# Reordering an attention and feed-forward kernel: every half pair begins with contexts, sums of weights earlier, GpSimd's additions later, the last scores between contexts

## The chip, the cores and the metric

The kernel runs on one core of a Trainium2 chip. A core has five engines that run side by side, each with a queue of instructions that it takes in order: TensorE (PE in the profile, with its weight loads as PEld), VectorE (DVE), ScalarE (ACT), GpSimd (POOL) and SyncE (SP, which here issues DMA transfers). An instruction that waits for another engine holds up everything behind it in its own queue. TensorE writes to PSUM, a small memory of eight banks; VectorE and ScalarE read it from there; GpSimd works on SBUF, the large on-chip memory. The metric is the device time of one execution in microseconds (us). Before the change it is 927.66 us, the median of three runs (926.39 to 928.1).

## The reference

Rows x (2048 rows of 640) are normalised, and the result xn goes two ways that are joined at the end. All tensors are bfloat16.

```python
xn = _layernorm(x, axis=-1)
q = (xn @ wq).reshape(B, Sq, 32, 192).transpose(0, 2, 1, 3)
k = k_cache[:, :, Sk - 512:, :]          # the last 512 keys of each of 32 heads
v = v_cache[:, :, Sk - 512:, :]
scores = jnp.einsum("bhqd,bhkd->bhqk", q, k) * (192 ** -0.5)
o = jnp.einsum("bhqk,bhkd->bhqd", _softmax(scores, axis=-1), v)
s = o.transpose(0, 2, 1, 3).reshape(B, Sq, 32 * 192) @ wo
g = _silu((_silu(xn @ w_gate) * (xn @ w_up)) @ w_down)
return x + s * g
```

## The kernel before

The feed-forward part with its result g comes first (to about 165 us). What follows is attention, in 16 *pairs* of heads, numbered 0 to 15 (`pr`). The 2048 queries are cut into four *blocks* of 512, and a pair is done in two *halves* of two blocks each. A block of a pair has the number i = 4 * pair + block. The order of the work on each engine is written out by hand: instructions run in the order in which the Python code issues them.

**Scores phase** (`scores_phase`, L924). A half begins with eight scores, two blocks by four chunks of 128 keys (`scores`, L592). A score is six matmuls into a PSUM tile `sc` (of which there are two, used in turn), and an exponential on ScalarE (L601) that empties it into `p_t`. Between the scores, at numbered slots 0 to 7, stand the products that make the queries of the *next* half: `differences`, `sides`, `across`, `sums` and `third` (`q_group`, L554). They use two more PSUM tiles, `mm`, which VectorE or ScalarE empties. The third product of a block is reduced by VectorE at L534 (`q_rows`). `sides` ends in a copy on ScalarE (L573); `across` adds on VectorE (L576), then subtracts at L581, on GpSimd for the pairs 0 to 14 and on VectorE for pair 15; `sums` ends at L586. In the first half of a pair two more things prepare the next pair: `combine_wq` (L136, three VectorE instructions at L143 that add and subtract weights) at slot 5, and `q_diag` (L548) at slot 7, a product that needs one of those sums and whose PSUM tile VectorE copies out at L552.

**Beside it** (`beside`, L905) run the preparations of the next pair's keys: transposing DMAs in the first half; in the second, sums over keys on VectorE (L174) at slots 0 to 2, and the *key centring* (`centre_k`, L180: five VectorE instructions at L186 that write `khat`) at slots 4 to 7.

**Stretch.** After the scores of a half comes a stretch of two kinds of work, in an order written as a string (`FIRST`, `LATER`, L884). Each name has a block of the half (0 and 1, or 2 and 3), a letter and a step 0 or 1:

- a and b are *contexts*, the products of `p_t` with the values (`pv`, L604), a for the first two query tiles of a block and b for the other two. They accumulate in an `mm` tile, taken at step 0. Each step is 16 matmuls of 64 rows, of which two run at once in two halves of the array. Between the steps the halves change PSUM banks, which is kept in order by a one-element `turn_t` memset in GpSimd's queue (L726): step 1 waits for it. After step 1 `divide` (L636) takes reciprocals on VectorE (L641), divides on ScalarE (L652; some parts on VectorE, L646) and issues a transposing DMA (L655).
- w, x and y are the *output products* with wo for the block two before, i - 2 (`wo_units`, L781): w0, w1, x0, x1 (`wo_turn`, L733, also with a turn between its steps) and y0 (`rest`). They use `sc` tiles, which VectorE adds to the running sums s_m and s_t (L752).

The first half of a later pair begins 0a0 0b0 0y0 0x0; its second half begins 2w0 2a0 2w1 2b0. Pair 0 has orders of its own.

**The end.** Pair 14 has no such string: `pv_full` and `wo_full` (L660, L808) do contexts and output products with matmuls of 128 rows. After the output product `gate` multiplies finished sums by g on GpSimd (L768), and `add_x` (L770, L779) adds x, in three instructions for each block: block 2 after the first half of pair 14, block 3 right after the scores of its second half, block 0 after the scores of pair 15's first half, all on GpSimd; block 1 on VectorE. Pair 15 does the scores of blocks 0 and 1 as above. Those of blocks 2 and 3 (s20 to s33) stand between the contexts of blocks 0 and 1 as `LAST` says. Then `pv_full`, `last_rows` and `last_rest` alternate until the stores.

Of the kernel before, what the change touches and what calls it, by code (L numbers as in the profile page):

```python
# [15 lines left out]
def kernel(  # L16
# [28 lines left out]
    NB = Sq // 512  # L45
# [90 lines left out]
    def combine_wq(pr):  # L136

        w = pairs[pr]["wq"]
        wc = pairs[pr]["wc"] = w[:, :, :, :].bitcast(h16)
        for to, a, b, op in (  # L140
            (TOTAL, SWAP, OTHER, ALU.add), (SWAP, SWAP, OWN, ALU.add), (OTHER, OTHER, OWN, ALU.subtract)
        ):
            nc.vector.tensor_tensor(wc[:, to, :, :], w[:, a, :, :], w[:, b, :, :], op)  # L143
# [57 lines left out]
    with ExitStack() as fctx:  # L201
# [238 lines left out]
        for b in range(NB):  # L440
# [3 lines left out]
            u = 0  # L444
# [72 lines left out]
    last = NPAIR - 1  # L517
    Ps, OTs, Obs, xbs = {}, {}, {}, {}
# [85 lines left out]
    def pv(i, q2):  # L604

        pr, b = divmod(i, NB)
        st = {}

        def part(p):
            if p == 0:  # L610
                if i not in OTs:
                    Obs[i] = opool.tile([P, 4, 2, Dh], bf, name="O_b")
                    tag = "OT_l" if late(i) and pr < last else "OT_b"
                    OTs[i] = otpool.tile([P, 12, P], bf, name=tag, tag=tag, bufs=2 if tag == "OT_l" else 3)
                st["acc"] = sc_tile() if i < 2 and q2 else mm_tile()
            acc = st["acc"]
            turn, h = divmod(p, 2)
            for kc in range(KC):
                for n, r in enumerate((lo, hi)):
                    k = n ^ turn  # L620
                    qt = 2 * q2 + k
                    m = nc.tensor.matmul(  # L622
                        acc[:, k, h * 256 : h * 256 + Dh + 1],
                        Ps[i][kc][r, h, qt * P : (qt + 1) * P], V_p[r, kc, h, 0 : Dh + 1],
                        start=(p == 0 and kc == 0), stop=(turn == 1 and kc == KC - 1),
                        skip_group_check=True,
                    )
                    after(m, st)
            if p == 1:
                turned(m, st)  # L630
            if p == 3:
                divide(i, q2, acc, (0, 1) if q2 == i else (0,) if pr == last else ())

        return [lambda t=t: (part(2 * t), part(2 * t + 1)) for t in range(2)]

    def divide(i, q2, acc, by_dve):  # L636
        pr, b = divmod(i, NB)
        O_b, OT_b = Obs[i], OTs[i]
        r = smpool.tile([P, 2, 2, 1], f32, name="r")
        a_v = acc[:, :, :].rearrange("p k (h c) -> p k h c", h=2)  # L640
        nc.vector.reciprocal(r[:], a_v[:, :, :, Dh : Dh + 1])  # L641
        for k in range(2):
            qt = 2 * q2 + k
            a_k = a_v[:, k, :, :]
            if by_dve and k in by_dve:
                nc.vector.tensor_tensor(  # L646
                    O_b[:, qt, :, :], a_k[:, :, 0:Dh], r[:, k, :, :].to_broadcast([P, 2, Dh]),
                    ALU.mult,
                )
                continue  # L650
            for h in range(2):
                nc.scalar.activation(  # L652
                    O_b[:, qt, h, :], a_k[:, h, 0:Dh], ACT.Copy, scale=r[:, k, h, :]
                )
        nc.sync.dma_start_transpose(  # L655
            out=OT_b[:, 6 * q2 : 6 * q2 + 6, :],
            in_=O_b[:, 2 * q2 : 2 * q2 + 2, :, :].rearrange("p t h d -> p (t h d)"),
        )

    def pv_full(i, q2):  # L660

        pr, b = divmod(i, NB)
        if q2 == 0:
            Obs[i] = opool.tile([P, 4, 2, Dh], bf, name="O_b")
            tag = "OT_l" if late(i) and pr < last else "OT_b"
            OTs[i] = otpool.tile([P, 12, P], bf, name=tag, tag=tag, bufs=2 if tag == "OT_l" else 3)
        O_b, OT_b = Obs[i], OTs[i]
        alone = pr == last and 2 * b + q2 < 5
        acc = mm_tile()
        for k in range(2):  # L670
            qt = 2 * q2 + k
            for h in range(2):
                for kc in range(KC):
                    nc.tensor.matmul(  # L674
                        acc[:, k, h * 256 : h * 256 + Dh + 1],
                        Ps[i][kc][:, h, qt * P : (qt + 1) * P], V_p[:, kc, h, 0 : Dh + 1],
                        start=(kc == 0), stop=(kc == KC - 1),
                    )
        divide(i, q2, acc, alone and (0,))

    def load_xb(b):

# [87 lines left out]
    def add_x(b, eng):  # L770
        for qts in (slice(0, 2), slice(2, 4), None):
            add_part(b, qts, eng)
# [8 lines left out]
    def wo_units(i):  # L781


        pr, b = divmod(i, NB)

        def unit(half):
            st = {}

            def first():
                st["sc"] = sc_tile()  # L790
                wo_turn(st, i, half, 0)

            def second():
                wo_turn(st, i, half, 1)
                sum_rows(i, slice(2 * half, 2 * half + 2), st["sc"][:, :, :])

            return [first, second]

        def rest():
            sc = sc_tile()  # L800
            for n, r in enumerate((lo, hi)):
                wo_rest(sc[:, n, :], i, r)
            for n in range(2):
                add_sum(pr + n, s_t[:, b, :], sc[:, n, :])

        return [unit(0), unit(1), [rest]]
# [72 lines left out]
    def store(left):  # L879
# [1 line left out]
            t, ob = stores.pop(0)  # L881
            nc.sync.dma_start(out=out2[t * P : (t + 1) * P, :], in_=ob)

    FIRST = ("0a0 0b0 0a1 0b1 1a0 1b0 1a1 1b1", "2a0 2b0 2w0 2w1 2a1 2y0 2x0 2b1 2x1 3w0 3a0 3w1 3b0 3y0 3a1 3x0 3b1 3x1")  # L884
    LATER = (
        "0a0 0b0 0y0 0x0 0a1 0x1 0w0 0b1 0w1 1w0 1b0 1w1 1a0 1b1 1y0 1x0 1a1 1x1",
        "2w0 2a0 2w1 2b0 2a1 2y0 2x0 2b1 2x1 3w0 3b0 3w1 3a0 3b1 3y0 3x0 3a1 3x1",
    )
    LAST = "s20 0a0 s21 0b0 0a1 0b1 s22 1a0 s23 1b0 s30 1a1 s31 1b1 s32 s33"

    def units_of(pr, bs):
        units = {}
        for b in bs:
            i = pr * NB + b
            units.update({"%da" % b: pv(i, 0), "%db" % b: pv(i, 1)})
            if i >= 2 and pr < last:
                units.update({"%d%s" % (b, n): u for n, u in zip("wxy", wo_units(i - 2))})
        return units

    def stretch(pr, half):  # L900
        units = units_of(pr, (2 * half, 2 * half + 1))
        for name in (LATER if pr else FIRST)[half].split():
            units[name[:2]][int(name[2])]()

    def beside(pr, n):  # L905
# [18 lines left out]
    def scores_phase(pr, half):  # L924


        nxt = pr + 1 < NPAIR
        if half == 0 and pr == 0:
            work = [lambda i=i, j=j: q_rows(i, j) for i in (2, 3) for j in range(3)]
            slots = {0: work[0:1], 1: work[1:2], 3: work[2:3], 4: work[3:4], 5: work[4:5], 6: work[5:6]}  # L930
        elif half == 0 or nxt:
            of = pr if half == 0 else pr + 1
            differences, sides, across, sums, third = q_group(of, 1 - half)
            slots = {
                0: [differences], 1: [sides], 3: [across, lambda: third(0)], 4: [sums],
                6: [lambda: third(1)],
            }
        if half == 0 and nxt:
            slots.setdefault(7, []).append(lambda: q_diag(pr + 1))
            slots.setdefault(5, []).insert(0, lambda: combine_wq(pr + 1))  # L940
        for n in range(2 * KC):
            for do in slots.get(n, ()):
                do()
            scores(pr * NB + 2 * half + n // KC, n % KC)
            beside(pr, 2 * half * KC + n)
            if pr >= last - 1 and (pr, half, n) in XB_AT:
                load_xb(XB_AT[pr, half, n])

    XB_AT = {(last - 1, 0, 7): 2, (last - 1, 1, 0): 3, (last - 1, 1, 4): 0, (last, 0, 0): 1}
    V, G = nc.vector, nc.gpsimd  # L950

    for pr in range(last):
        for half in range(2):
            scores_phase(pr, half)
            if pr == last - 1 and half:
                add_x(3, G)
            if pr < last - 1:
                stretch(pr, half)
                continue
            for b in (2 * half, 2 * half + 1):  # L960
                i = pr * NB + b
                for q2 in range(2):
                    pv_full(i, q2)
                    wo_full(i - 2, q2)
            if half == 0:
                add_x(2, G)
# [1 line left out]
    add_x(0, G)  # L968
    add_x(1, V)
    i = last * NB  # L970
    units = units_of(last, (0, 1))
    for name in LAST.split():
        if name[0] == "s":
            scores(i + int(name[1]), int(name[2]))
# [3 lines left out]
        m_f[:, 0, :, :], m_f[:, 1, :, :],  # L978
        xc[:, SUM + 1, 0:4, :].rearrange("p c n -> p (c n)").bitcast(f32).rearrange("p (t d) -> p t d", d=512),
    ]  # L980
    pv_full(i + 2, 0)
    for b, q2, more in ((0, 0, (2, 1)), (0, 1, (3, 0)), (1, 0, (3, 1)), (1, 1, None)):
        last_rows(b, slice(2 * q2, 2 * q2 + 2), G, sc_tile)
        if q2:
# [47 lines left out]
```

## Time and profile before

| | |
|---|---|
| median of three runs | 927.66 us (926.39 to 928.1) |
| the profiled execution | 927.22 us |
| its span, first to last instruction | 925.4 us |
| busy, TensorE | 905.7 us (98%) |
| busy, VectorE | 583.3 us (63%) |
| busy, ScalarE | 501.6 us (54%) |
| busy, GpSimd | 148.5 us (16%) |
| mean granted TensorE clock | 0.998 |
| one pair (2 to 13), start to start | 46.9 us |

Busy time of TensorE includes the pipelined tail of each matmul, so rows overlap: a row of six score matmuls shows 0.83 us, but the row behind it starts 0.65 us after it. Where TensorE has work waiting, six matmuls of 64 rows by 512 columns take 0.65 us from start to start of rows, ten 1.08 us, a context step (x16) 0.67 us and two of them (x32) 1.33 us. With this a wait is read from the starts of two rows in the timeline: what lies between them, less what the first needs.

### The profile page before, as it was taken

The numbers are of one execution on the slowest core, as the hardware profiler recorded it, in microseconds if no ns is written. First come the engines' busy times: TensorE is split into PE (matmuls) and PEld (weight loads), VectorE is DVE, ScalarE is ACT, GpSimd is POOL, SyncE is SP. The second block draws the span as 40 slices with busy tenths as digits, with TensorE's granted clock in tenths as the row PEclk, the third lists the DMA queues.
The fourth block names the chain that finished last, engine by engine and source line by source line (L and its number), as shares of the span: only waits on it lengthen the run. The fifth ranks groups of instructions, "written<-read, shape, count | busy, mean of one in ns | idle before, by whom it ended". The sixth has DMA issues, their size and how long they took to land.

```text
span 925.4 us, 23283 instructions
## 1 busy us (share of the span) xinstructions
PE 905.7 (98%) x9797; PEld 539.4 (58%) x9819; DVE 583.3 (63%) x862; ACT 501.6 (54%) x873; POOL 148.5 (16%) x298
## 2 busy tenths in 40 slices
PE   9999999999999999999999999999999999999898
PEld 5444444465656666666666666666665666665565
DVE  6443552465767676767676767676766676767657
ACT  4222222566656566656566666666656656566471
POOL 0000000011111111111111111111111111116826
PEclk9999999999999999999999999999999999999999
DMA  9313460054444444455444444444444453544336
GB/s 301 75 35 91 97 123 0 1 91 88 81 85 81 92 81 91 81 91 83 91 81 91 81 91 81 91 82 91 77 88 85 76 94 78 91 80 111 67 87 163
DMA packets 266025, 81.98 MB, mean 89 GB/s; under 512 B 244928, under 2 KB 265920, under 8 KB 265920
## 3 DMA queue, kind: packets, MB, share of 16 engines
q1 hardware_dynamic: 263552, 77.82, 42.5%
q10 hardware_dynamic: 2368, 2.67, 0.9%
q8 instruction: 77, 1.26, 0.6%
q14 instruction: 28, 0.23, 0.1%
HBM read 41.39 MB, written 2.62 MB: 48 GB/s over the span
## 4 chain that ended last, share of the span: by engine, by line
PE 82%; DVE 7%; ACT 3%; DMA 2%; issue 2%; POOL 2%; SPq 1%; DVEq 0%; ACTq 0%; POOLq 0%
PE mm L622 15%; PE sc L739 15%; PE sc L597 11%; PE sc L315 11%; PE mm L543 9%; PE mm L345 6%; PE mm L529 5%; PE sc L709 4%; PE sc L701 2%; DVE wq_p L143 2%; PE mm L674 2%; DVE qT L534 2%; ACT p_t L601 2%; DVE m_f L552 2%; POOL m_f L581 2%
## 5 line engine op out<-in xcount | busy, mean ns | idle before, releaser
L601 ACT ACTIVATE p_t<-sc 128x1024 bf16<-128x1024 f32 x256 | 253.9, 1025 | 81.5 <-PE sc L597 81.3
L652 ACT ACTIVATE O_b<-mm,r 128x192 bf16<-128x192 f32 x490 | 166.2, 422 | 198.6 <-issue 125.4
L597 PE MATMUL sc<-qT,khat 64*128 64x512 bf16 x1536 | 197.4, 376 | 1.2 <-ACT p_t L601 1.2
L622 PEld LDWEIGHTS <-p_t 64*128 64x128 bf16 x3712 | 164.6, 94 | 39.3 <-issue 4.0
L622 PE MATMUL mm<-V_p,p_t 64*128 64x193 bf16 x3648 | 184.9, 243 | 1.7 <-ACT O_b L652 0.4
L739 PE MATMUL sc<-wo_p,OT_b 64*128 64x512 bf16 x1296 | 171.3, 376 | 7.1 <-ACT p_t L601 6.8
L752 DVE TENSOR_TENSOR s_m<-s_m,sc 128x1024 f32<-128x1024 f32 x108 | 131.9, 1221 | 71.4 <-PE sc L739 63.3
L597 PEld LDWEIGHTS <-khat 64*128 64x128 bf16 x1536 | 87.4, 94 | 78.4 <-issue 1.8
L739 PEld LDWEIGHTS <-OT_b 64*128 64x128 bf16 x1296 | 69.5, 94 | 54.5 <-issue 11.0
L726 POOL MEMSET turn_t<- 128x1 f32 x224 | 22.2, 99 | 477.5 <-PE mm L622 249.4
L752 DVE TENSOR_TENSOR s_t<-s_t,sc 128x512 f32<-128x512 f32 x108 | 74.2, 687 | 38.8 <-PE sc L709 36.9
L534 DVE TENSOR_REDUCE qT<-mm 128x512 bf16<-128x1024 f32 x66 | 80.6, 1222 | 26.2 <-PE mm L529 23.3
L543 PE MATMUL mm<-xc,wq_p 64*128 64x512 f16 x750 | 94.2, 376 | 0.4 <-ACT O_b L652 0.4
L581 POOL TENSOR_TENSOR m_f<-m_f 128x1024 f32<-128x1024 f32 x28 | 65.8, 2349 | 178.4 <-DVE qT L576 172.1
L543 PEld LDWEIGHTS <-wq_p 64*128 64x128 f16 (+1 forms) x1050 | 56.3, 94 | 58.2 <-DVE wq_p L143 5.1
L529 PE MATMUL mm<-xnT,wq_p 64*128 64x512 bf16 x660 | 82.9, 376 | 0.2 <-ACT m_f L573 0.2
L323 DVE TENSOR_TENSOR hT<-sc,sg 128x512 bf16<-128x512 f32 x46 | 31.7, 691 | 70.2 <-ACT sg L322 70.2
L576 DVE TENSOR_TENSOR qT<-mm,m_f 128x1024 bf16<-128x1024 f32 x30 | 36.7, 1224 | 56.6 <-ACT m_f L573 56.6
L322 ACT ACTIVATE sg<-sc 128x512 bf16<-128x512 f32 x46 | 27.3, 597 | 69.8 <-PE sc L315 65.1
L315 PE MATMUL sc<-xnT,wg_sb 128*128 128x512 bf16 (+1 forms) x255 | 59.9, 354 | 1.4 <-DMA wg_sb<-in_B_w_gate_dram 0.7
L315 PE MATMUL sc<-xnT,wu_sb 128*128 128x512 bf16 (+1 forms) x255 | 59.4, 354 | 0.2
L529 PEld LDWEIGHTS <-wq_p 64*128 64x128 bf16 x660 | 35.9, 94 | 37.1 <-issue 5.7
(96 smaller groups left out, 720.6 us busy)
## 6 DMA issues: line engine op xcount, KB each, us to landing
wo_p<-in_A_wo_dram SPq DMA_DIRECT2D x16, 480.0 KB, 3.8
wq_p<-in_A_wq_dram SPq DMA_DIRECT2D x79, 80.0 KB, 2.9
K_p<-in_A_k_cache_dram SPq DMA_DIRECT2D x32, 192.0 KB, 3.1
V_p<-in_A_v_cache_dram SPq DMA_DIRECT2D x32, 192.0 KB, 3.1
wq_p<-in_A_wq_dram SPq DMA_DIRECT2D x90, 40.0 KB, 2.6
x_t<-in_A_x_dram SPq DMA_DIRECT2D x13, 160.0 KB, 2.9
xc<-in_A_x_dram SPq DMA_DIRECT2D x4, 512.0 KB, 4.3
OT_b<-O_b SPq DMA_TRANSPOSE x124, 2.8
```

What stands on the lines that cost most here:

```text
L315: nc.tensor.matmul(out, w_sb[:, c, f * P : (f + 1) * P], xnT[:, c, qc], start=(c == 0), stop=(c == NC - 1),)
L345: nc.tensor.matmul(dn, at, by, start=(f == 0), stop=(f == NF - 1))
L529: nc.tensor.matmul(q_ps[:, h, :], w[r, AS_IS[j], c, :], xnT[r, c, b * 512 : (b + 1) * 512], start=(c == 0), stop=(c == NC - 1),)
L534: nc.vector.reduce_sum(q_of(i, j), q_ps[:, :, :].rearrange("p h n -> p n h"), axis=AX.X)
L543: nc.tensor.matmul(ps[:, h, :], ws[h][r, c, :], xs[h][r, c, :], start=(first and c == 0), stop=(c == NC - 1), skip_group_check=True,)
L581: eng.tensor_tensor(m_f[:, SIDE_S, :, :], diag, m_f[:, SIDE_S, :, :], ALU.subtract)
L597: nc.tensor.matmul(sc[:, h, :], khat[r, j, ks], q_of(i, j)[r, :], start=(j == 0), stop=(j == 2))
L601: nc.scalar.activation(p_t[:, :, :], sc[:, :, :], ACT.Exp, scale=scale)
L622: m = nc.tensor.matmul(acc[:, k, h * 256 : h * 256 + Dh + 1], Ps[i][kc][r, h, qt * P : (qt + 1) * P], V_p[r, kc, h, 0 : Dh + 1], start=(p ...
L652: nc.scalar.activation(O_b[:, qt, h, :], a_k[:, h, 0:Dh], ACT.Copy, scale=r[:, k, h, :])
L739: m = nc.tensor.matmul(ps[:, k, :], OTs[i][r, 3 * (2 * half + k) + j, :], pairs[i // NB]["wo"][r, j, MAIN], start=(turn == 0 and j == 0), ...
L752: nc.vector.tensor_tensor(to, to, ps, ALU.add)
```

## The change

Both halves of every later pair, and the second half of pair 0, use the one order that the first half had, which begins with contexts; `combine_wq` goes from slot 5 to slot 2 of the first half; `add_x(3, G)`, three GpSimd instructions, goes from ahead of pair 14's last contexts and output products to a place between them, behind the first `gate`; `LAST` begins with a context instead of a score, and takes the first contexts of block 2 in two steps, one ahead of the last score and one behind it, where `pv_full(i + 2, 0)` had followed all scores. The same computation is done with the same instructions, but for those contexts, which become 32 matmuls of 64 rows and one more memset in place of 16 of 128 rows.

```diff
--- before.py
+++ after.py
@@ -660,12 +660,11 @@
     def pv_full(i, q2):
 
         pr, b = divmod(i, NB)
-        if q2 == 0:
+        if i not in OTs:
             Obs[i] = opool.tile([P, 4, 2, Dh], bf, name="O_b")
             tag = "OT_l" if late(i) and pr < last else "OT_b"
             OTs[i] = otpool.tile([P, 12, P], bf, name=tag, tag=tag, bufs=2 if tag == "OT_l" else 3)
         O_b, OT_b = Obs[i], OTs[i]
-        alone = pr == last and 2 * b + q2 < 5
         acc = mm_tile()
         for k in range(2):
             qt = 2 * q2 + k
@@ -676,7 +675,7 @@
                         Ps[i][kc][:, h, qt * P : (qt + 1) * P], V_p[:, kc, h, 0 : Dh + 1],
                         start=(kc == 0), stop=(kc == KC - 1),
                     )
-        divide(i, q2, acc, alone and (0,))
+        divide(i, q2, acc, ())
 
     def load_xb(b):
 
@@ -881,25 +880,22 @@
             t, ob = stores.pop(0)
             nc.sync.dma_start(out=out2[t * P : (t + 1) * P, :], in_=ob)
 
-    FIRST = ("0a0 0b0 0a1 0b1 1a0 1b0 1a1 1b1", "2a0 2b0 2w0 2w1 2a1 2y0 2x0 2b1 2x1 3w0 3a0 3w1 3b0 3y0 3a1 3x0 3b1 3x1")
-    LATER = (
-        "0a0 0b0 0y0 0x0 0a1 0x1 0w0 0b1 0w1 1w0 1b0 1w1 1a0 1b1 1y0 1x0 1a1 1x1",
-        "2w0 2a0 2w1 2b0 2a1 2y0 2x0 2b1 2x1 3w0 3b0 3w1 3a0 3b1 3y0 3x0 3a1 3x1",
-    )
-    LAST = "s20 0a0 s21 0b0 0a1 0b1 s22 1a0 s23 1b0 s30 1a1 s31 1b1 s32 s33"
-
-    def units_of(pr, bs):
+    FIRST = "0a0 0b0 0a1 0b1 1a0 1b0 1a1 1b1"
+    LATER = "0a0 0b0 0y0 0x0 0a1 0x1 0w0 0b1 0w1 1w0 1b0 1w1 1a0 1b1 1y0 1x0 1a1 1x1"
+    LAST = "0a0 s20 0b0 s21 0a1 0b1 s22 1a0 s23 1b0 s30 1a1 s31 1b1 s32 2a0 s33 2a1"
+
+    def units_of(i, n):
         units = {}
-        for b in bs:
-            i = pr * NB + b
-            units.update({"%da" % b: pv(i, 0), "%db" % b: pv(i, 1)})
-            if i >= 2 and pr < last:
-                units.update({"%d%s" % (b, n): u for n, u in zip("wxy", wo_units(i - 2))})
+        for k in range(n):
+            units.update({"%da" % k: pv(i + k, 0), "%db" % k: pv(i + k, 1)})
+            if 2 <= i < last * NB:
+                units.update({"%d%s" % (k, n): u for n, u in zip("wxy", wo_units(i + k - 2))})
         return units
 
     def stretch(pr, half):
-        units = units_of(pr, (2 * half, 2 * half + 1))
-        for name in (LATER if pr else FIRST)[half].split():
+        i = pr * NB + 2 * half
+        units = units_of(i, 2)
+        for name in (LATER if i else FIRST).split():
             units[name[:2]][int(name[2])]()
 
     def beside(pr, n):
@@ -937,7 +933,7 @@
             }
         if half == 0 and nxt:
             slots.setdefault(7, []).append(lambda: q_diag(pr + 1))
-            slots.setdefault(5, []).insert(0, lambda: combine_wq(pr + 1))
+            slots.setdefault(2, []).append(lambda: combine_wq(pr + 1))
         for n in range(2 * KC):
             for do in slots.get(n, ()):
                 do()
@@ -952,8 +948,6 @@
     for pr in range(last):
         for half in range(2):
             scores_phase(pr, half)
-            if pr == last - 1 and half:
-                add_x(3, G)
             if pr < last - 1:
                 stretch(pr, half)
                 continue
@@ -961,6 +955,8 @@
                 i = pr * NB + b
                 for q2 in range(2):
                     pv_full(i, q2)
+                    if b == 2 and q2:
+                        add_x(3, G)
                     wo_full(i - 2, q2)
             if half == 0:
                 add_x(2, G)
@@ -968,7 +964,7 @@
     add_x(0, G)
     add_x(1, V)
     i = last * NB
-    units = units_of(last, (0, 1))
+    units = units_of(i, 3)
     for name in LAST.split():
         if name[0] == "s":
             scores(i + int(name[1]), int(name[2]))
@@ -978,7 +974,6 @@
         m_f[:, 0, :, :], m_f[:, 1, :, :],
         xc[:, SUM + 1, 0:4, :].rearrange("p c n -> p (c n)").bitcast(f32).rearrange("p (t d) -> p t d", d=512),
     ]
-    pv_full(i + 2, 0)
     for b, q2, more in ((0, 0, (2, 1)), (0, 1, (3, 0)), (1, 0, (3, 1)), (1, 1, None)):
         last_rows(b, slice(2 * q2, 2 * q2 + 2), G, sc_tile)
         if q2:
```

## The prediction

> **What bounds the kernel now.** I read the page first, for whether one engine carries the whole span.
>
> ```profile
> PE 905.7 (98%) x9797; PEld 539.4 (58%) x9819; DVE 583.3 (63%) x862; ACT 501.6 (54%) x873; POOL 148.5 (16%) x298
> PE   9999999999999999999999999999999999999898
> ```
>
> TensorE is the bound in every slice, and VectorE and ScalarE have a third to a half of their time free. What can be gained without taking matmuls away is the time in which TensorE waits, so I went through its timeline and compared the starts of rows with the 0.65 us of six matmuls, 1.08 us of ten and 0.67 us of a context step. One pair, from the timeline of TensorE (start, duration, engine, line, count, idle before):
>
> ```profile
> 433.27 1.47 PE L597 MATMUL sc<-qT,khat 64*128 64x512 bf16 x12
> 435.27 0.82 PE L739 MATMUL sc<-wo_p,OT_b 64*128 64x512 bf16 x6 [0.52 <-ACT p_t L601]
> ...
> 457.09 1.25 PE L543 MATMUL mm<-xc,wq_p 64*128 64x512 f16 x10
> 458.18 0.81 PE L597 MATMUL sc<-qT,khat 64*128 64x512 bf16 x6
> 458.82 1.77 PE L622 MATMUL mm<-V_p,p_t 64*128 64x193 bf16 x32
> 460.41 0.83 PE L709 MATMUL sc<-OT_b,wo_p 64*128 64x512 bf16 x6
> ```
>
> At 433.27 two scores need 1.29, so 434.56; the output product starts at 435.27. TensorE waits 0.71 us there, since w0 needs the tile of the seventh score, whose exponential is late. At 458.82 two context steps take 1.59 and not 1.33: 0.26-0.28 us between 0a0 and 0b0. What holds 0b0 is in VectorE's timeline:
>
> ```profile
> 433.85 1.22 DVE L534 TENSOR_REDUCE qT<-mm 128x512 bf16<-128x1024 f32 x1
> 435.10 1.08 DVE L186 TENSOR_SCALAR khat<-KT,nmean 128x512 bf16<-128x512 bf16 x3
> ...
> 456.03 1.41 DVE L143 TENSOR_TENSOR wq_p<-wq_p 128x640 f16<-128x640 bf16 x3
> 457.35 1.22 DVE L534 TENSOR_REDUCE qT<-mm 128x512 bf16<-128x1024 f32 x1
> 458.49 1.21 DVE L552 COPY m_f<-mm 128x1024 f32<-128x1024 f32 x1
> ```
>
> The copy of q_diag's tile ends at 459.70, after the three sums of weights and a reduction. The waits summed over the kernel say how often the first one comes:
>
> ```profile
> PE sc L739 <- ACT p_t L601: 6.8, 13, 0.5
> ```
>
> Thirteen times: the second halves of pairs 1 to 13. The other large wait is in pair 14. TensorE, VectorE and GpSimd there:
>
> ```profile
> 858.81 1.46 PE L701 MATMUL sc<-wo_p,OT_b 128*128 128x512 bf16 x5
> 862.58 2.75 PE L674 MATMUL mm<-V_p,p_t 128*128 128x193 bf16 x16 [2.31 <-DVE qT L534]
> 865.12 1.79 PE L701 MATMUL sc<-wo_p,OT_b 128*128 128x512 bf16 x6
> ```
>
> ```profile
> 851.99 1.81 DVE L581 TENSOR_TENSOR m_f<-m_f 128x1024 f32<-128x1024 f32 x1
> ...
> 856.97 4.31 DVE L186 TENSOR_SCALAR khat<-KT,nmean 64x512 bf16<-64x512 bf16 x2
> 861.30 1.23 DVE L534 TENSOR_REDUCE qT<-mm 128x512 bf16<-128x1024 f32 x1
> ```
>
> ```profile
> 850.58 5.21 POOL L779 TENSOR_TENSOR s_m<-s_m,xc 128x1024 f32<-128x1024 f32 x2
> ...
> 856.87 4.25 POOL L779 TENSOR_TENSOR s_m<-s_m,xc 128x1024 f32<-128x1024 f32 x2
> ...
> 877.36 5.20 POOL L779 TENSOR_TENSOR s_m<-s_m,xc 128x1024 f32<-128x1024 f32 x2
> ```
>
> Two key centrings take 4.31 us beside add_x(3), where 0.71 is what two take elsewhere (433.10). The reduction behind them ends at 862.5, and the next context, which needs its tile, starts 3.77 us after the row at 858.81 where 1.30 would do: a wait of 2.47. After it TensorE is slow: 16 matmuls take 2.54 us to the next row instead of 1.33, the next six 1.63 instead of 1.30. The granted clock from 862.58 to 866.75 is 0.62. So the wait costs 2.47 + 1.21 + 0.33 = 4.0 us.
>
> **The change part by part**, against the profiled execution's 927.22 us (its span of 925.4 and 1.8 around it).
>
> *Contexts first in pairs 1 to 13.* The second half now starts 0a0 0b0 at 434.56. 0a0's tile was read by `sums`, which ended at 432.98; 0b0, at 435.23, needs the reduction that ends at 435.07. y0 then comes at 435.89 and needs the seventh score's exponential; ScalarE starts it at 434.20 and ends it at 435.2. x0 at 436.54 needs the eighth, ended at 436.14. VectorE is through with the key centring at 436.18, y0's sums reach it at 436.75, and w0 at 438.5 needs the tile that they free at 438.1. Nothing is late by these rows, though by only 0.16, 0.4 and 0.4 us. Gain 13 x 0.71 = 9.2 us. Downward bound: 0b0 late by what the first half shows, 0.28, leaves 5.6.
>
> *Pair 0's second half.* Its own order has three waits: 200.53 to 201.64 for six matmuls (0.46, a turn), 202.96 to 203.78 (0.17), 210.99 to 212.23 (0.59, the first product of pair 1 waits for a division). The common order shows none of them in later pairs, and a wait of 0.15 at 248.0 in pair 1, w1 behind 2a0, goes too. Gain 1.35; between 0.8 (the division still late) and 1.4.
>
> *Sums of weights at slot 2.* VectorE is idle there from 448.51 to 451.20, until ScalarE's copy lets `across` start; the three instructions (1.41 us) fit, and GpSimd's product at L581 comes only after them. Then the reduction starts when TensorE has ended the third product, 456.60, and ends at 457.8, and the copy waits for q_diag alone. q_diag itself comes 0.05 earlier, since its weight load no longer waits for a sum. The copy can start 0.21 us after the last matmul (as the reduction at 883.04 does), at 458.33 and not 458.49. So only 0.16 of the 0.27 goes; the copy's own 1.21 us stay between. Gain 13 x 0.16 = 2.1; from 0.65 (the 0.05 alone) to 3.6 (all of it).
>
> *GpSimd's x later, pair 14.* add_x(3) now stands behind a gate that waits for VectorE, so GpSimd is idle from 856.9 while the key centring runs at 0.36 us each: reduction from 857.7 to 858.9, and the context at 860.10 does not wait. Gain 4.0. [...]
>
> *What is queued behind it.* GpSimd's order in pair 14 becomes gate, add_x(3), five gates, add_x(0), then the turns of pair 15. The first gate waits for the sum that VectorE can start at 860.3 and ends 2.13 us after its own start at 861.6. By their rows: 2.13 + 5.4 (4.25 + 1.21) + 2.13 + 1.17 + 2.13 + 2.13 + 1.17 = 16.3, so 877.9, and add_x(0) to 883.3. TensorE meanwhile has gained 4.0, ends pair 15's first eight scores at 880.1, and with 0a0 s20 0b0 s21 (2.64 us) comes to 0a1 at 882.7, whose turn is behind add_x(0). Add_x(0) now also runs beside VectorE's add_x(1), and the rows say what that costs: two parts of add_x take 5.21 and 5.20 when VectorE's L581 falls into them, 4.25 when not, 0.95 for each VectorE instruction with both operands in SBUF; VectorE's own goes from 1.17 to 1.81. With L581 and one or two parts of add_x(1) in the way GpSimd ends 1.9 to 2.9 later, 885.2 to 886.2. TensorE waits about 3.0 us, and the divisions behind the delayed add_x(1) come some 0.7 late for 1a0: cost 3.7. Bounds: 0.6 (no meeting on SBUF) and 5.9 (3.5 + 0.8, and then half speed as after 862.58, 1.5). [...]
>
> *The last scores.* Before, s20 waits 0.71 (882.83 to 884.83 for two scores), 1a0 0.61 (888.79 to 890.05), s33 0.81 (894.66 to 896.12), together 2.1. In the new order every score has 1.3 us between it and the last but one, which is more than an exponential's 1.03, and eight of these with eight divided parts (8 x 1.03 + 4 x 0.75 = 11.2 us of ScalarE) fit beside 8 x 0.65 + 10 x 0.67 = 11.9 us of TensorE. Contexts in steps of 64 rows take as long as 16 matmuls of 128 rows (1.33 both). Gain 2.1; if ScalarE, delayed by the turn, makes TensorE wait, 1.0. Behind this TensorE runs without waits to 921.9, so what is won here reaches the end.
>
> Sum: 9.2 + 1.35 + 2.1 + 4.0 - 3.7 + 2.1 = 15.1. 927.22 - 15.1 = 912.1; the median of the runs lies 0.44 above the profiled one, so I forecast 912.2 for the median.
>
> **The rivals.** *GpSimd doesn't hold TensorE up.* If add_x(0) is not slowed, the turn comes at 883.4 and the cost is 0.6: 909.1. For it: GpSimd's 4.25 us beside the two slowed centrings shows no delay of its own. Against: two rows of 5.2.
>
> *A small wait at the head of the second half.* 0b0 has a margin of 0.16 us, and the first half shows 0.28 of wait in the same place. Then 13 x 0.28 = 3.6 come back: 915.8. *The sums of weights do nothing*, the copy being what is late: 912.2 + 1.5 = 913.7.
>
> *Slower than before: the key centring slowed in every second half.* It stands ahead of the reduction that 0b0 now needs 0.67 us after the scores. Were it slowed as in pair 14 (4.31 instead of 0.71), 0b0 would wait 3.4 us, 13 x 3.4 = 44, and the total would be 956. It decides from 15.1 / 13 = 1.2 us of wait in each half on. Against it: GpSimd is through with L581 at 431.7, 1.4 us before the centring, and idle to 436.2.
>
> **How the numbers follow.** Forecast, with GpSimd late by 2 to 4 us: 56%. GpSimd hardly late: 20%. Small wait at the second halves: 11%. Sums of weights without effect: 8%. Slower: 4%, and 1% for no change. Best bounds together: 9.2 + 1.4 + 3.6 + 4.0 - 0.6 + 2.1 = 19.7, so 907.5; the worst without a new wait in each half: 9.2 + 0.8 + 0.65 + 4.0 - 5.9 + 1.0 = 9.8, so 917.4. I take 907.5 to 917.5, which leaves out a mix of late GpSimd and new waits, and the slower case. A measurement of this kernel can tell about 0.2%, 1.9 us, from no change; by the cases faster has 95%, same 1%, slower 4%.
>
> **What would show it.** Right: the row for PE L739 waiting on the exponential disappears from the waits; second halves begin with x32 of L622 right behind the scores; the 1.59 of the first halves becomes about 1.43; in pair 14 each centring takes 0.36 us, and no clock below 0.9 stands behind it; in pair 15 a wait of L622 on `turn_t`, 2 to 4 us, comes after s21. Wrong: a wait of L622 on L534 or L709 on a sum in each second half, another period than 46.9 - 0.87 = 46.1 us, or pair 15 without the wait for GpSimd.

## The result, and the profile after

The changed kernel takes 913.11 us (median of four runs, 912.78 to 913.35) against 927.32 us before (four runs, 926.39 to 928.1): a ratio of 0.9847, with a 95% interval of 0.983 to 0.9864. Its profiled execution takes 913.02 us, its span is 911.2. The forecast was 912.2, the range 907.5 to 917.5.

The page of the changed kernel, first the engines, then TensorE by slices:

```profile
PE 902.4 (99%) x9835; PEld 543.1 (60%) x9835; DVE 585.6 (64%) x862; ACT 501.2 (55%) x873; POOL 149.0 (16%) x299
PE   9999999999999999999999999999999999999988
```

The work is the same and TensorE is still the bound; what went is waiting. The heads of two stretches in TensorE's timeline of the changed kernel (start, duration, engine, line, count):

```profile
429.10 1.47 PE L597 MATMUL sc<-qT,khat 64*128 64x512 bf16 x12
430.40 1.51 PE L622 MATMUL mm<-V_p,p_t 64*128 64x193 bf16 x32
431.73 0.83 PE L708 MATMUL sc<-OT_b,wo_p 64*128 64x512 bf16 x6
...
453.25 0.83 PE L597 MATMUL sc<-qT,khat 64*128 64x512 bf16 x6
453.89 1.69 PE L622 MATMUL mm<-V_p,p_t 64*128 64x193 bf16 x32
455.41 0.83 PE L708 MATMUL sc<-OT_b,wo_p 64*128 64x512 bf16 x6
```

At 430.40 a second half: two context steps follow the scores at once and take 1.33 us, with no wait before or between. At 453.89 a first half: 1.52 us, so 0.19 us of its wait is left. What leaves it there is seen in VectorE's timeline:

```profile
443.56 1.41 DVE L143 TENSOR_TENSOR wq_p<-wq_p 128x640 f16<-128x640 bf16 x3
...
451.74 1.22 DVE L534 TENSOR_REDUCE qT<-mm 128x512 bf16<-128x1024 f32 x1 [0.51 <-PE mm L529]
453.46 1.23 DVE L552 COPY m_f<-mm 128x1024 f32<-128x1024 f32 x1 [0.50 <-PE mm L543]
```

The sums of weights end 7 us before the product at 452.17 that needs them; the copy at L552 now waits for its product and ends at 454.7, while 0b0 could begin at 454.56. In pair 14 the two key centrings take 0.71 us, and the second context follows the output product after 1.30 us, at 848.45. From here on the new wait of the forecast is found. VectorE, GpSimd and TensorE of the changed kernel in pairs 14 and 15:

```profile
845.30 0.71 DVE L186 TENSOR_SCALAR khat<-KT,nmean 64x512 bf16<-64x512 bf16 x2
...
863.05 2.77 DVE L581 TENSOR_TENSOR m_f<-m_f 128x1024 f32<-128x1024 f32 x1
...
869.44 4.75 DVE L778 TENSOR_TENSOR s_m<-s_m,xc 128x1024 f32<-128x1024 f32 x2
874.11 0.68 DVE L778 TENSOR_TENSOR s_t<-s_t,xT 128x512 f32<-128x512 f32 x1
```

```profile
849.95 2.13 POOL L767 TENSOR_TENSOR s_m<-s_m,g_m 128x1024 f32<-128x1024 f32 x1 [4.71 <-DVE s_m L751]
...
860.51 4.22 POOL L767 TENSOR_TENSOR s_m<-s_m,g_m 128x1024 f32<-128x1024 f32 x2
864.68 2.15 POOL L767 TENSOR_TENSOR s_t<-s_t,g_t 128x512 f32<-128x512 f32 x1
866.79 4.22 POOL L778 TENSOR_TENSOR s_m<-s_m,xc 128x1024 f32<-128x1024 f32 x2
870.97 2.13 POOL L778 TENSOR_TENSOR s_t<-s_t,xT 128x512 f32<-128x512 f32 x1
873.04 0.25 POOL L725 MEMSET turn_t<- 128x1 f32 x2
```

```profile
845.81 1.51 PE L673 MATMUL mm<-V_p,p_t 128*128 128x193 bf16 x16
847.15 1.46 PE L700 MATMUL sc<-wo_p,OT_b 128*128 128x512 bf16 x6
848.45 1.50 PE L673 MATMUL mm<-V_p,p_t 128*128 128x193 bf16 x16
...
867.00 1.26 PE L529 MATMUL mm<-xnT,wq_p 64*128 64x512 bf16 x10 [0.90 <-DVE qT L534]
...
871.39 0.83 PE L597 MATMUL sc<-qT,khat 64*128 64x512 bf16 x6
873.19 1.51 PE L622 MATMUL mm<-V_p,p_t 64*128 64x193 bf16 x32 [0.98 <-POOL turn_t L725]
874.54 0.81 PE L597 MATMUL sc<-qT,khat 64*128 64x512 bf16 x6
876.41 0.84 PE L622 MATMUL mm<-V_p,p_t 64*128 64x193 bf16 x16 [1.06 <-ACT O_b L652]
```

The kernel before, at the places that are compared with these:

```profile
878.72 1.84 DVE L581 TENSOR_TENSOR m_f<-m_f 128x1024 f32<-128x1024 f32 x1
...
884.19 2.35 DVE L779 TENSOR_TENSOR s_m<-s_m,xc 128x1024 f32<-128x1024 f32 x2
```

```profile
882.51 1.16 POOL L779 TENSOR_TENSOR s_t<-s_t,xT 128x512 f32<-128x512 f32 x1
```

In the changed kernel GpSimd is busy without a pause from 849.95 until the first turn at 873.04. VectorE's L581 falls into its gates and takes 2.77 us instead of the 1.84 it took before, so the reduction behind it is late, and the third product at 867.00 waits 1.1 us. 0a1 at 873.19 starts 1.80 us after the score at 871.39, which needs 0.65, so it waits 1.16 for the turn. VectorE's x for block 1 takes 4.75 us for two parts, where it took 2.35, the divisions come late, and 1a0 at 876.41 waits 1.22 us.

By parts, from the first score of a pair to the first of the next half or pair (starts of rows in TensorE's timelines of the two profiled executions; the first half of pair 0 takes 18.07 us in both):

| part | before, us | after, us | difference | forecast |
|---|---|---|---|---|
| up to the first score (not changed) | 171.61 | 172.13 | +0.5 | 0 |
| pair 0, second half | 23.63 | 22.60 | -1.0 | -1.2 |
| pair 1, second half | 23.28 | 22.42 | -0.9 | -0.9 |
| pairs 2 to 13, second halves | 12 x 23.12 (one 23.41) | 12 x 22.42 (one 22.70) | -8.4 | -8.5 |
| pairs 1 to 13, first halves | 13 x 23.82 | 13 x 23.68 | -1.8 | -2.1 |
| pair 14 | 50.56 | 46.48 | -4.1 | -4.0 |
| pair 15 and the end of the span | 50.94 | 52.39 | +1.5 | +1.6 |
| span | 925.4 | 911.2 | -14.2 | -15.1 |

### The profile page after: what moved, and what is told of

It is laid out like the page before. It is cut to its first block, busy times and chain, and to the rows that moved or that the text cites. A ratio compares the mean times of both kernels' runs of the same rounds, so it can differ in the third digit from the quotient of the medians.

```text
span 911.2 us, 23325 instructions
## 1 busy us (share of the span) xinstructions
PE 902.4 (99%) x9835; PEld 543.1 (60%) x9835; DVE 585.6 (64%) x862; ACT 501.2 (55%) x873; POOL 149.0 (16%) x299
## 4 chain that ended last, share of the span: by engine, by line
PE 94%; POOL 3%; issue 1%; DMA 1%; DVE 1%; ACT 0%; ACTq 0%; POOLq 0%
PE mm L622 17%; PE sc L597 16%; PE sc L738 15%; PE mm L543 12%; PE sc L315 11%; PE mm L529 7%; PE mm L345 6%; PE sc L708 4%; PE sc L700 2%; POOL s_m L778 1%; PE mm L673 1%; POOL s_m L767 1%; PE mm L700 1%; PE mm L352 1%; DMA x_t<-in_A_x_dram 1%
## 5 line engine op out<-in xcount | busy, mean ns | idle before, releaser
L601 ACT ACTIVATE p_t<-sc 128x1024 bf16<-128x1024 f32 x256 | 253.8, 1024 | 81.9 <-PE sc L597 81.7
L622 PE MATMUL mm<-V_p,p_t 64*128 64x193 bf16 x3680 | 186.9, 243 | 2.1 <-ACT O_b L652 1.1
L738 PE MATMUL sc<-wo_p,OT_b 64*128 64x512 bf16 x1296 | 169.1, 376 | 0.0
L581 POOL TENSOR_TENSOR m_f<-m_f 128x1024 f32<-128x1024 f32 x28 | 65.7, 2348 | 177.8 <-DVE qT L576 171.5
L543 PEld LDWEIGHTS <-wq_p 64*128 64x128 f16 (+1 forms) x1050 | 58.7, 94 | 54.5 <-issue 0.8
```

The lines of the kernel that those rows point to most:

```text
L543: nc.tensor.matmul(ps[:, h, :], ws[h][r, c, :], xs[h][r, c, :], start=(first and c == 0), stop=(c == NC - 1), skip_group_check=True,)
L581: eng.tensor_tensor(m_f[:, SIDE_S, :, :], diag, m_f[:, SIDE_S, :, :], ALU.subtract)
L601: nc.scalar.activation(p_t[:, :, :], sc[:, :, :], ACT.Exp, scale=scale)
L622: m = nc.tensor.matmul(acc[:, k, h * 256 : h * 256 + Dh + 1], Ps[i][kc][r, h, qt * P : (qt + 1) * P], V_p[r, kc, h, 0 : Dh + 1], start=(p ...
L738: m = nc.tensor.matmul(ps[:, k, :], OTs[i][r, 3 * (2 * half + k) + j, :], pairs[i // NB]["wo"][r, j, MAIN], start=(turn == 0 and j == 0), ...
```

## The experiments

Two questions were open after this. Does each edit alone do what its term says? And are the three waits of pair 15 GpSimd's queue, as forecast, or the new order of the last scores? Four kernels take one edit each into the kernel before; the others change the changed kernel.

**The common order alone.**

```diff
-        "2w0 2a0 2w1 2b0 2a1 2y0 2x0 2b1 2x1 3w0 3b0 3w1 3a0 3b1 3y0 3x0 3a1 3x1",
+        "2a0 2b0 2y0 2x0 2a1 2x1 2w0 2b1 2w1 3w0 3b0 3w1 3a0 3b1 3y0 3x0 3a1 3x1",
...
-        for name in (LATER if pr else FIRST)[half].split():
+        for name in (LATER if pr or half else FIRST)[half].split():
```

> The kernel before with the common order in both halves alone (also in pair 0's second half). Theory, by what the changed kernel's trace shows of this part: 13 waits of 0.70 us, 0.15 in pair 1 and 1.0 in pair 0 go, 10.2 us, so about 917.1. Rival, that VectorE's key centring holds the second context back where the sums of weights still stand late: 13 x 0.28 comes back, about 920.7. In the trace, second halves start with two context steps in 1.33 us (theory) or 1.6 us (rival).

Measured: 915.33 us (915.03 to 916.95) against 926.85 (27 runs), ratio 0.9883 (0.9865 to 0.9901). All second halves of pairs 1 to 13 take 22.42 us, one 22.72, so the 10.3 us are there and the rival is not. The median moved by 11.5, more than the order explains. The rest stands in pair 14, which this edit does not touch: TensorE waits there as in the kernel before, but does not become slow. Its timeline, then the window behind the wait (columns: window, its length, busy time of each engine, granted clock, DMA share, GB/s):

```profile
848.07 1.46 PE L701 MATMUL sc<-wo_p,OT_b 128*128 128x512 bf16 x5
851.84 1.49 PE L674 MATMUL mm<-V_p,p_t 128*128 128x193 bf16 x16 [2.31 <-DVE qT L534]
853.17 1.46 PE L701 MATMUL sc<-wo_p,OT_b 128*128 128x512 bf16 x6
```

```profile
851.80:856.00 4.20, 4.16 (x36) 3.10 (x36) 3.77 (x8) 2.60 (x8) 1.70 (x1) 1.00 0.05 10
```

and the same window of the kernel before:

```profile
862.50:866.70 4.20, 4.12 (x22) 3.05 (x22) 2.55 (x7) 2.48 (x8) 1.66 (x1) 0.61 0.04 8
```

The same 3.77 us from row to row, the same wait of 2.47; the 16 matmuls behind it take 1.33 us at a granted clock of 1.00 here and 2.54 at 0.61 there. The slow clock is no fixed price of the wait. The mean granted clock is on record for every execution: three of the four here have 0.999 or 1.0 (915.03 to 915.39 us) and one 0.998 (916.95); of the 27 of the kernel before, 13 have 0.999 or 1.0 (median 925.75) and 14 have 0.997 or 0.998 (median 927.41). Between executions of full clock the order is worth 10.5 us, near the 10.3 of the halves.

**The sums of weights alone.**

```diff
-            slots.setdefault(5, []).insert(0, lambda: combine_wq(pr + 1))
+            slots.setdefault(2, []).append(lambda: combine_wq(pr + 1))
```

> The kernel before with the sums of weights at slot 2 alone. Theory: the copy of the product that needs the sums can start about 0.1 us earlier and the product itself 0.05, since the copy's own 1.2 us stay; 13 x 0.14 = 1.8 us, about 925.5, and the two context steps at the head of a first half go from 1.59 to about 1.51 us. Rival one, the copy alone is late: 13 x 0.05, 926.7. Rival two, the sums are the whole wait: 13 x 0.28, 923.7.

Measured: 923.98 us (11 runs, 923.31 to 926.0), ratio 0.998 (0.997 to 0.999). First halves of pairs 1 to 13 take 23.68 us instead of 23.82, 13 x 0.14 = 1.8 us, and the two context steps 1.51 us, as the theory has it. Its profiled execution, 925.32 us, is 1.9 below that of the kernel before, and has the slow clock in pair 14 too (0.60 from 860.5 to 864.7). Of the eleven times four lie at 925.3 to 926.0 and seven at 923.3 to 924.1 with none between. The four are those with a mean granted clock of 0.998, the seven those with 0.999 or 1.0, so the median by itself can't price this edit. Against the kernel before in executions of the same clock it gains 1.6 us (medians 927.41 and 925.86) and 1.9 (925.75 and 923.86), which fits the 1.8 of the halves.

**GpSimd's x alone** (`add_x(3, G)` behind the second context of pair 14's block 2, as in the change).

> The kernel before with GpSimd's x for block 3 moved behind the first gate alone. Theory: in pair 14 the wait of 2.47 us and the slow clock after it go, 4.0 us; then GpSimd's queue runs into pair 15 as in the changed kernel, VectorE's x for block 1 is blocked by it and the divisions come late, so that 1a0 starts some 2 us later than it would; net 2.0, about 925.3. Rival, that the queue does no harm in the old order of pair 15 because its first turn is asked for later: 923.3.

Measured: 924.95 us (11 runs, 924.54 to 925.66), ratio 0.9982 (0.9973 to 0.9991). Pair 14's second half falls from 26.78 to 22.76, and pair 15 with the end grows from 50.94 to 53.0: 4.0 gained, 2.1 lost. In TensorE's timeline the third product waits 1.1 us, 0a1 0.5 for the turn, 1a0 1.2. The queue does its harm in the old order too. All eleven executions have a mean granted clock of 0.999 or 1.0: with the wait of pair 14 the slow clock is gone.

**The new order of the last pair alone** (`LAST`, `units_of` with block 2, no `pv_full(i + 2, 0)`).

> The kernel before with the new order of the last pair alone. Theory: the waits of s20, 1a0 and s33 (2.1 us) go and about 0.4 of waits for ScalarE stays; GpSimd is through at 883.7 and the first turn is asked for at 886.8, so it holds nothing up: 1.8 us, about 925.5. Rival, that the new order itself makes the waits of pair 15 that the changed kernel shows (1.1, 1.2 and 1.2 us): about 1.4 us slower than before, 928.7.

Measured: 925.91 us (11 runs, 924.2 to 926.67), ratio 0.9984 (0.9974 to 0.9993). Pair 15 with the end takes 49.74 instead of 50.94, so the order gains 1.2 us. s20 and s33 no longer wait their 0.7 and 0.8, but 1a0 waits 0.62 as before, s33 waits 0.15, and the first output product comes 0.23 late, where the step from matmuls of 64 rows to matmuls of 128 alone took 0.11 in the kernel before (896.12 to 896.88). No wait for a turn, none of over 0.2 at the third product: the new order is not what makes them.

**Less in GpSimd's queue, in two ways.** In the first the addition is moved once more:

```diff
-                    if b == 2 and q2:
-                        add_x(3, G)
...
+    add_x(3, G)
     s_fs += [
```

> The changed kernel with GpSimd's x for block 3 moved once more, behind the last pair's scores and contexts, ahead of the final output products. Theory: the backlog of GpSimd in pair 15 is the cause of its three waits (1.08 at the third product, 1.16 at the turn, 1.24 at 1a0); with 5.4 us less in the queue they go, 3.5 us, about 909.6. At the end GpSimd has to do the three additions beside the final ones, whose gaps there add up to some 5 us, so up to 1 us may come back. Rival, that the waits belong to the new order of the last scores: about 913.1, or later where the end becomes GpSimd's.

In the second it is left out:

> The changed kernel without the addition of x to block 3 (the last 512 rows come out without x, so that GpSimd has three instructions, 5.4 us, less to do). Theory: the three waits of pair 15 go and nothing is added at the end, 909.6. Rival: 913.1.

Measured: 909.63 us (five runs, ratio 0.9818, 0.9804 to 0.9831) and 909.52 us (four runs, ratio 0.9816, 0.9802 to 0.9829). Pair 15 and the end take 49.71 and 49.72 us where the changed kernel has 52.39: the backlog costs 2.7 us, and three additions in the end's gaps cost nothing. That the time of 909.6 was met is partly luck: the theory had 3.5 us going in pair 15, and of the 3.6 and 3.5 us by which the profiled executions fell, 0.9 and 0.8 stand in the part up to the first score (171.20 and 171.33 us in these profiles, 172.13 in the changed kernel's). GpSimd of the first of them, and the largest wait that its TensorE has left in attention (in all, times, longest):

```profile
860.77 5.20 POOL L778 TENSOR_TENSOR s_m<-s_m,xc 128x1024 f32<-128x1024 f32 x2
865.93 1.15 POOL L778 TENSOR_TENSOR s_t<-s_t,xT 128x512 f32<-128x512 f32 x1
868.45 0.10 POOL L725 MEMSET turn_t<- 128x1 f32 x1 [1.37 <-PE mm L622]
...
879.08 4.22 POOL L778 TENSOR_TENSOR s_m<-s_m,xc 128x1024 f32<-128x1024 f32 x2
883.25 1.16 POOL L778 TENSOR_TENSOR s_t<-s_t,xT 128x512 f32<-128x512 f32 x1
```

```profile
PE mm L622 <- ACT O_b L652: 0.4, 1, 0.4
```

GpSimd is idle for 1.37 us before the first turn. 1a0 still waits 0.62, by the starts of its rows, so of its 1.22 in the changed kernel half belongs to the queue and half to the order, which at this place is the same before and after the change.

**More in GpSimd's queue.**

```diff
+    nc.gpsimd.tensor_tensor(m_f[:, 0, 0, :], m_f[:, 0, 1, :], m_f[:, 1, 1, :], ALU.add)
     for name in LAST.split():
```

> The changed kernel with one more GpSimd addition of 128x512, about 1.2 us, ahead of the turns of pair 15 (its result is not used). Theory: GpSimd sets the start of 0a1, so its wait grows from 1.16 to some 2.3 us, about 914.3; if a wait of that length brings the slow clock that the kernel before had after 2.47 us, another 1 to 1.5 us comes on top, 915.5, with a granted clock near 0.6 for three or four us. Rival, that the turn's wait is not GpSimd's length: 913.1.

Measured: 915.09 us (four runs, 914.25 to 915.46), ratio 0.9873 (0.986 to 0.9887). 0a1 now waits 3.36 us for the turn instead of 1.16, and 1a0 0.61 instead of 1.22; pair 15 with the end grows by 1.6 us, to 54.0. The wait grew by 2.2, more than the 1.2 that was reckoned for the added instruction. That it took longer beside VectorE's x is an estimate from the changed kernel, where another addition of 512 columns took 2.13 us there (at 870.97) and not 1.15. In the profiled execution (914.25 us, mean granted clock 0.999) no slow clock stands behind this wait, though it is longer than that of pair 14:

```profile
871.04 0.83 PE L597 MATMUL sc<-qT,khat 64*128 64x512 bf16 x6
875.05 1.51 PE L622 MATMUL mm<-V_p,p_t 64*128 64x193 bf16 x32 [3.18 <-POOL turn_t L725]
876.39 0.81 PE L597 MATMUL sc<-qT,khat 64*128 64x512 bf16 x6
```

```profile
875.00:879.20 4.20, 3.71 (x66) 2.88 (x68) 1.89 (x5) 2.27 (x5) 0.20 (x2) 1.00 0.11 23
```

The other three executions (914.9 to 915.46) have a mean clock of 0.998; that they had the slow clock behind this wait is likely, but no profile shows them.

**The product that needs the sums, one slot earlier.**

```diff
-            slots.setdefault(7, []).append(lambda: q_diag(pr + 1))
+            slots.setdefault(6 if pr else 7, []).append(lambda: q_diag(pr + 1))
```

> The changed kernel with the product that needs the sums of weights at slot 6, behind the third product, and not at slot 7 (pairs 1 to 14). Theory: what is left of the wait at the head of first halves, 0.18 us, is the 1.2 us copy of that product, which then starts 0.65 us earlier: 13 x 0.18 = 2.3 us, about 910.8, and the two context steps take 1.33 us. Rival: two scores then follow each other without work between, as in second halves, and ScalarE makes a later unit wait 0.2 us or more: 913 or above.

Measured: 909.99 us (four runs, 909.93 to 910.98), ratio 0.9822 (0.9809 to 0.9836). First halves of pairs 1 to 13 take 23.50 instead of 23.68, 13 x 0.18 = 2.3 us, and the two context steps 1.33; the rival is not there. Most of the rest of the 3.1 by which the median fell lies, by the profiles, in the part up to the first score, which took 171.41 in this one and 172.13 in the changed kernel's.

**Both, and one step on.** The two edits together, then also s23 ahead of 1a0, and the changed kernel again beside them on one chip:

```diff
-    LAST = "0a0 s20 0b0 s21 0a1 0b1 s22 1a0 s23 1b0 s30 1a1 s31 1b1 s32 2a0 s33 2a1"
+    LAST = "0a0 s20 0b0 s21 0a1 0b1 s22 s23 1a0 1b0 s30 1a1 s31 1b1 s32 2a0 s33 2a1"
```

> The changed kernel with both edits, GpSimd's x for block 3 behind the last scores and the product that needs the sums at slot 6. Theory: the two gains touch different waits and add up, 2.3 + 3.5 - 0.8 (what is left of pair 15's waits in the run without the backlog) = about 5.0 us below the changed kernel, 907.9 or a little less. Rival: one of the two was a gain of its chip or of its start, and the sum stays above 909.

> The same with s23 ahead of 1a0 in the order of the last pair. Theory: the 0.62 us that 1a0 waits for the division of 0a is filled by a score, so 0.6 less than the kernel with both edits, about 907. Rival: s22 and s23 back to back make ScalarE's exponentials the wait, for s30 or later, and the 0.6 comes back: about 907.9.

> The changed kernel as it is, once more beside the two others on one chip: 913.1, with a spread under 1 us, since no wait of it is followed by a slow clock.

Measured: 907.12 us (five runs, ratio 0.9792, 0.9779 to 0.9806), 907.11 (four runs, ratio 0.9789, 0.9775 to 0.9803), and 912.75 for the changed kernel (five runs, 912.45 to 913.27, ratio 0.985, 0.9836 to 0.9864). The two gains add up: from the first score to the end of the span, 739.1 us in the changed kernel's repeat and 734.1 with both. The order with s23 first takes 0.45 off pair 15 (49.27 instead of 49.72), where 1a0 no longer waits and s30 waits 0.18; in the times the two can't be told apart. Both are faster than either kernel of the case.

## Why the prediction was right

*Contexts first.* The term was 13 x 0.71 = 9.2 and is 13 x 0.70 = 9.1. The three thin margins that it was read from, 0.16, 0.4 and 0.4 us, held in all thirteen pairs, so that neither the small wait nor the slowed key centring of the rivals appears; first and second halves together take 46.10 us, the forecast's 46.1.

*Pair 0.* 1.35 with the 0.15 of pair 1; measured 1.2, since 0.19 of wait came up between two output products.

*Sums of weights.* 2.1, measured 1.8. The step that decided, that the copy's own 1.2 us stay, is what the profile after shows and what the kernel with the product one slot earlier confirms: there the 0.18 are gone. The rival that the sums do nothing falls. The sign that the 1.59 of the first halves becomes about 1.43 was off: it became 1.52, since 0.05 us of the gain stands ahead of the product that needs the sums and only 0.07 between the contexts.

*GpSimd's x, pair 14.* 4.0, and the profiled executions differ by that (26.78 and 22.75 us for the second half of pair 14). But 1.5 of it was taken for a fixed price of the wait, and that is wrong. The common order alone, with the same 2.47 us wait, ran on at a granted clock of 1.00 (851.8 to 856.0), and of 44 executions of the kernel before that ran beside the experiments 24 have a mean granted clock of 0.997 or 0.998 (median 927.26 us) and 20 one of 0.999 or 1.0 (925.84). Against the first the term is 4.0, against the second 2.5; that the profile which the prediction was made from was of the first kind is chance. The length of the idle time does not decide either: 2.31 us was followed by the slow clock in three profiles, 3.18 us was not in another. What decides is not shown by these runs.

*GpSimd's queue and the last scores.* Cost 3.7 less gain 2.1 was +1.6; measured +1.5. That this term came out is luck, since the sum hides two misses of about 1 us each. The gain was 1.2: the prediction counted 1a0's wait of 0.61 as going, though "0a1 0b1 s22 1a0", which sets it, is the same in both orders, and it left out the 0.3 that ScalarE makes TensorE wait at the end (its lower bound of 1.0 had that). The cost was 2.7. That GpSimd would be late was right: pair 14's second half starts 11.64 us earlier in the changed kernel (836.06 and 847.70), so that the reckoning's first gate at 861.6 is to be looked for at 849.96, and its turn, 885.2 to 886.2, at 873.6 to 874.6; measured were 849.95 and 873.04. But 1.1 of it was met by TensorE already at the third product (0.14 of that stood there before), because L581 took 2.77 us on VectorE and not 1.84; the prediction had put the whole wait at the turn. With this its sign of recognition, a wait of 2 to 4 us on `turn_t`, failed: it was 1.16.

*The sum.* 15.1 forecast, 14.2 measured in the profiled executions. 0.5 of the difference is the part up to the first score, which nothing in the change touches and which took between 171.09 and 172.13 us over the profiles here; 0.2 and 0.3 come from pair 0 and from the sums of weights. Against executions of the kernel before at full clock the gain is about 12.7 us (925.84 less 913.11).

## What to carry to other kernels

When an engine is busy 98% of the time, compare the starts of its rows with what the same count of instructions takes elsewhere: the waits found in this way priced this reordering to a microsecond before it ran, though two of the terms were off by a microsecond each, in opposite directions. When work is moved off a stall, follow its new place to the end of that engine's queue and ask who waits there for something small; here the longer queue cost 2.7 of the 4 us won, 1.2 of them at a one-element memset, and moving three additions into the idle time of the end brought the 2.7 back. Price a wait by its length, and treat a slow clock behind it as something that may come in some executions only: here 35 of the 70 executions with pair 14's wait had a mean granted clock of 0.998 or less.

## What the runs showed of the hardware

The wait of 2.47 us in pair 14, with 2.31 us in which TensorE is idle, was followed by a slow clock in three profiles and by none in a fourth. In the kernel before the granted clock is 0.50 from 862.38 to 865.79 and 1.00 ahead of it and behind it (the first figures: the window, its length, TensorE's busy time; third from the end: the granted clock):

```profile
858.97:862.38 3.41, 1.25 (x6) 0.49 (x5) 3.36 (x3) 0.00 (x0) 3.32 (x3) 1.00 0.00 0
862.38:865.79 3.41, 3.21 (x18) 2.66 (x18) 2.67 (x7) 1.56 (x5) 0.75 (x1) 0.50 0.00 0
865.79:869.20 3.41, 3.41 (x27) 2.25 (x26) 2.00 (x3) 1.15 (x4) 2.33 (x2) 1.00 0.60 115
```

At the same place the sums of weights alone had 0.60 over 4.20 us (860.5 to 864.7), the new order alone 0.59 (862.6 to 866.8), and the common order alone 1.00 (851.8 to 856.0). The wait of 3.36 us in the kernel with the longer queue of GpSimd, 3.18 of it idle, was followed by 1.00 (875.0 to 879.2) in the one profile of it. So in these five profiles the longer of the two idle times was not followed by the slow clock, and the shorter one was in three of four; what sets this is not shown here.

How often the slow clock came is seen in the mean granted clock of each execution: of the four kernels with pair 14's wait 70 executions have it on record, and 35 of them have 0.998 or less, while all eleven of GpSimd's x alone, which has no such wait, have 0.999 or 1.0. The kernels that keep pair 14's wait spread over about 2.5 us in eleven runs (923.31 to 926.0, 924.2 to 926.67), the one without it over 1.1.

In the changed kernel VectorE and GpSimd both took longer where additions with both operands in SBUF ran side by side. VectorE's two parts of x took 4.75 us beside GpSimd, and 2.35 alone in the kernel before; GpSimd's two parts of 512 columns took 2.15 and 2.13 instead of 1.16 and 1.15, while its parts of 1024 columns took the usual 2.11 each. An addition with one operand in PSUM was not slowed: L586 took 1.21 us at 866.87 in the changed kernel, beside GpSimd, and 1.22 at 431.76 in the kernel before, where GpSimd was idle. In GpSimd's queue the two longer parts make 2.0 us, 1.0 each; the prediction had reckoned with 1.9 to 2.9.
